# Chunk attention and a multiplicative FFN on one core: 512-column products for part of the first four pairs, and a new hand-written order of loads and steps

## The chip, the cores and the metric

The kernel runs on one core of a Trainium2 chip. The metric is the device time in microseconds of one execution; three executions of the kernel before gave 242.46, 243.07 and 241.17 us, with a median of 242.46 us. A profiled execution is a separate one; all times inside the kernel come from it.

## What is computed

For 8 batches, 8 heads and 576 rows of 64 elements, attention runs inside chunks of 64 rows; the heads are put side by side to rows of 512; then comes a feed-forward part with four weights. Cut to what matters:

```
scores = q_c @ k_c.T / sqrt(64)          # per chunk of 64 rows
attn   = exp(scores) / sum(exp(scores))
x      = (attn @ v_c) as [4608, 512]
a, b   = x @ w1, x @ w2                  # each [4608, 1024]
out    = ((a * b) @ w3) @ w_out          # [4608, 512]
```

The inputs are float32, the products run in bfloat16, and the result is float32. The kernel multiplies w3 by w_out once (w3o), and uses that product for all rows.

## The kernel before, in words

The 4608 rows are 18 **pairs** of 256 rows (p = 0 to 17); two pairs make a **couple** (g = p // 2) of 512 rows. The work is a list of named steps, the string `ORDER`: each step is a letter with its numbers, and a loop at the end of `first_path` calls one small function for each. Every instruction is kept in that order on its engine, so `ORDER` fixes, engine by engine, what stands behind what; semaphores between the engines do the rest. Matrix products are all recorded at L97 and loads at L100, in helpers.

The steps of a pair p, in the order in which the data flow:

- `q`, `k`, `v`: loads from HBM with a cast to bfloat16, issued from POOL's queue (pair 0's q and k come by `R` over the SP and ACT queues as float32 and are cast by ACT in `K`). A pair's q or k is 256 KB in bfloat16, a v too. `i0` to `i3` load quarters of w1 and w2, 256 KB each, `h0`, `h1` halves of w3, `o` all of w_out. POOL's queue holds a limited number of loads: a later one is issued when an earlier one has landed.
- `T p.0`, `T p.1` (L207, DVE): block transposes of q and k.
- `G g.0`, `G g.1` (L199, SP's queue, from pair 6 on): eight transfers inside the chip that spread a couple's transposed q and k over the partitions, so that scores take fewer matmuls.
- `S` (PE): scores, 64 small matmuls, 32 from pair 6 on. `E` (ACT, L240): the exponential. `P` (PE): attention times v, with the row sums as one more column. `N` (DVE, L269 and L272): reciprocal and multiplication, two halves. `X` (DVE, L305 or L313): transposes of the result.
- `H g.0`, `H g.1` (L199, SP's queue, couples 3 to 8): eight transfers that bring a couple's transposed x into place; `A` and `B` of that couple read it.
- `A p.j` and `B p.j` (PE): x @ w1 and x @ w2. From pair 4 on one step makes 128 of the 1024 columns (f = j) for both pairs of the couple: 4 matmuls of 512 columns, written under the couple's even pair. For pairs 0 to 3 one step makes 256 columns (f = 2j and 2j+1) for one pair: 8 matmuls of 256 columns. `C` (ACT, L370) copies the first product out of PSUM, `M` (DVE, L387) multiplies it by the second.
- `O` (PE): 16 matmuls with w3o for a pair's output (24 smaller ones for the last). `Y` (ACT, L417) copies it out, `Q` (SP's queue) stores it.

`V` (DVE), `W` (PE) and `Z` (ACT) make w3o. `D` (PE) are matmuls on zeros whose result nobody reads: nine of 512 columns at the start, then twice six. PSUM is four tiles of two banks for all of it, so a step that opens a tile waits for the reader of an older one. SP's queue, too, issues a transfer only when the eighth before it has landed.

The order of the kernel before around what changes, engine by engine:

```
PE:   D(9) S0.0 S0.1 P0.0 P0.1 D(6) S1 D(6) A0.0 P1 B0.0 A0.1 B0.1 A0.2 A1.0 B0.2 A1.1 B1.0 B1.1
      A0.3 S2 B0.3 P2 A1.2 A1.3 B1.2 B1.3 A2.0 B2.0 S3 A2.1 ...
      B4.7 P8 S9 O4 P9 O5 A6.0 ... B6.4 A6.5 S10 B6.5 A6.6 P10 S11 B6.6 A6.7 P11 B6.7 A8.0 ... B8.7 A10.0
DVE:  T0.0.0 T0.1.0 T0.0.1 T0.1.1 T1.0 N0.0 T1.1 N0.1 X0.0 X0.1 N1.0 X1.0 N1.1 M0.0 X1.1 M0.1 M0.2 T2.0 T2.1
      M1.0 M1.1 M0.3 N2.0 N2.1 X2.0 X2.1 T3.0 T3.1 ...
      M4.3 T10.1 M4.4 X7.1 M4.5 M4.6 M4.7 T11.0 N8.0 N8.1 T11.1 T12.0 X8.0 N9.0 ...
POOL: v0 q1 k1 i0 v1 i1 i2 q2 k2 i3 v2 q3 k3 q4 v3 k4 h0 o h1 q5 k5 v4 q6 k6 q7 k7 q8 v5 k8 q9 k9 q10 v6 v7
      k10 v8 q11 v9 k11 q12 k12 ...
SP:   G3 Q0 Q1 G4 Q2 Q3 H3 G5 H4 G6 Q4 H5 Q5 G7 H6 G8 ...
```

Of the kernel before, what the change touches and what calls it, by code (L numbers as in the profile page):

```python
# [7 lines left out]

ORDER = """
R0.0 R1.0 R0.1 R1.1 v0 D0.0.1.9.512 K0.0 K1.0 T0.0.0 K0.1 T0.1.0 K1.1 S0.0 T0.0.1 E0.0 T0.1.1 q1 k1  # L10
S0.1 i0 E0.1 P0.0 P0.1 T1.0 D0.1.0.6.512 v1 N0.0 T1.1 N0.1 X0.0 X0.1 i1 i2 S1 E1 D1.0.0.6.512 A0.0
C0.0 P1 B0.0 q2 N1.0 X1.0 N1.1 A0.1 C0.1 k2 B0.1 M0.0 A0.2 X1.1 A1.0 i3 C0.2 B0.2 M0.1 A1.1 v2 q3
B1.0 B1.1 M0.2 C1.0 C1.1 T2.0 k3 A0.3 C0.3 T2.1 S2 E2 B0.3 M1.0 M1.1 P2 M0.3 N2.0 N2.1 A1.2 C1.2
X2.0 A1.3 X2.1 C1.3 T3.0 B1.2 q4 T3.1 v3 k4 B1.3 A2.0 M1.2 C2.0 B2.0 S3 E3 T4.0 A2.1 M1.3 B2.1 M2.0
P3 A2.2 h0 N3.0 N3.1 B2.2 X3.0 A2.3 C2.1 C2.2 X3.1 o M2.1 C2.3 B2.3 A3.0 C3.0 M2.2 B3.0 V0 h1 A3.1
A3.2 q5 k5 C3.1 M2.3 B3.1 B3.2 v4 V1 C3.2 q6 T4.1 V2 V3 M3.0 W0 S4 k6 q7 M3.1 Z0 M3.2 V4 V5 W1 T5.0
Z1 W2 V6 V7 T5.1 W3 T6.0 E4 k7 q8 v5 Z2 A3.3 k8 q9 k9 Z3 S5 T6.1 T7.0 q10 T7.1 E5 v6 v7 C3.3 P4 B3.3
N4.0 X4.0 M3.3 O0 G3.0 N4.1 k10 Y0 G3.1 T8.0 O1 X4.1 P5 T8.1 Y1 O2 Q0 N5.0 N5.1 X5.0 v8 X5.1 A4.0 S6
E6 T9.0 T9.1 S7 B4.0 T10.0 Y2 q11 O3 C4.0 M4.0 Q1 E7 P6 v9 N6.0 A4.1 N6.1 C4.1 Y3 B4.1 A4.2 X6.0
M4.1 G4.0 A4.3 X6.1 C4.2 P7 N7.0 C4.3 B4.2 G4.1 k11 B4.3 N7.1 X7.0 A4.4 M4.2 B4.4 Q2 M4.3 C4.4 T10.1  # L20
M4.4 A4.5 C4.5 S8 B4.5 A4.6 C4.6 A4.7 E8 B4.6 Q3 C4.7 X7.1 B4.7 M4.5 q12 P8 H3.0 M4.6 S9 H3.1 M4.7
O4 E9 T11.0 Y4 P9 N8.0 O5 k12 N8.1 A6.0 B6.0 Y5 T11.1 G5.0 T12.0 A6.1 X8.0 N9.0 B6.1 C6.0 C6.1 T12.1
A6.2 q13 X8.1 B6.2 N9.1 X9.0 M6.0 k13 C6.2 v10 T13.0 v11 X9.1 M6.1 A6.3 M6.2 q14 G5.1 C6.3 A6.4 q15
B6.3 C6.4 B6.4 A6.5 S10 C6.5 B6.5 T13.1 M6.3 M6.4 A6.6 H4.0 E10 P10 H4.1 M6.5 S11 N10.0 B6.6 k14
N10.1 v12 A6.7 C6.6 E11 G6.0 P11 M6.6 N11.0 B6.7 X10.0 N11.1 A8.0 A8.1 B8.0 G6.1 C6.7 C8.0 B8.1 A8.2
B8.2 C8.1 M6.7 T14.0 q16 A8.3 M8.0 C8.2 M8.1 X10.1 M8.2 X11.0 Q4 q17 T14.1 H5.0 B8.3 C8.3 S12 S13
X11.1 A8.4 E12 C8.4 B8.4 k15 H5.1 M8.3 E13 v13 k16 A8.5 B8.5 P12 M8.4 k17 v14 T15.0 N12.0 N12.1 O6
A8.6 v15 C8.5 C8.6 T15.1 Y6 T16.0 B8.6 A8.7 M8.5 C8.7 P13 Q5 M8.6 B8.7 X12.0 A10.0 C10.0 B10.0 N13.0
N13.1 M8.7 G7.0 A10.1 T16.1 C10.1 A10.2 X12.1 X13.0 M10.0 C10.2 G7.1 B10.1 B10.2 A10.3 B10.3 C10.3
M10.1 T17.0 A10.4 C10.4 M10.2 M10.3 A10.5 T17.1 B10.4 M10.4 X13.1 v16 H6.0 S14 C10.5 S15 G8.0 B10.5  # L30
M10.5 O7 G8.1 E14 E15 P14 A10.6 H6.1 N14.0 C10.6 B10.6 A10.7 N14.1 Q6 Y7 M10.6 P15 N15.0 N15.1 C10.7
X14.0 S16 B10.7 M10.7 O8 E16 Q7 A12.0 B12.0 C12.0 M12.0 Y8 A12.1 C12.1 P16 S17 N16.0 X14.1 B12.1 E17
A12.2 M12.1 B12.2 A12.3 C12.2 A12.4 B12.3 X15.0 B12.4 v17 C12.3 M12.2 A12.5 N16.1 B12.5 M12.3 H7.0
X15.1 A12.6 X16.0 A12.7 C12.4 M12.4 C12.5 M12.5 C12.6 P17 N17.0 Q8 B12.6 B12.7 M12.6 H7.1 A14.0
A14.1 C12.7 B14.0 N17.1 C14.0 M12.7 O9 B14.1 C14.1 Y9 A14.2 X16.1 M14.0 M14.1 C14.2 A14.3 B14.2 Q9
O10 B14.3 X17.0 H8.0 Y10 Q10 A14.4 C14.3 A14.5 X17.1 C14.4 B14.4 M14.2 B14.5 H8.1 M14.3 A14.6 O11
Y11 B14.6 M14.4 O12 C14.5 C14.6 Y12 A14.7 M14.5 A16.0 C14.7 C16.0 Q11 M14.6 B14.7 A16.1 C16.1 A16.2
B16.0 B16.1 M14.7 M16.0 C16.2 M16.1 Q12 A16.3 O13 B16.2 B16.3 A16.4 C16.3 M16.2 Y13 M16.3 C16.4
A16.5 A16.6 B16.4 A16.7 C16.5 B16.5 M16.4 O14 Y14 C16.6 B16.6 C16.7 M16.5 B16.7 M16.6 Q13 M16.7 O15
Y15 O16 Q14 Q15 Y16 Q16 O17  # L40
"""


# [5 lines left out]
def first_path(  # L49
# [46 lines left out]
    def mm(*a, **kw):
        return inorder(nc.tensor.matmul(*a, **kw))  # L97
# [276 lines left out]
    def do_M(p, j):  # L374
        g = p // 2
        if g not in ab_t:
            ab_t[g] = msb.tile([P, FO, GT], bf, tag="ab", bufs=3, name="ab")
# [9 lines left out]
        inorder(nc.vector.tensor_mul(o, view(a_t.pop((p, j))[:]), view(ps_t.pop((p, j))[:, 1, :])))  # L387
# [201 lines left out]
```

## Time and profile before

| | before |
|---|---|
| time of the profiled execution | 241.66 us |
| its span, first to last instruction | 240.1 us |
| median of three other executions | 242.46 us |
| PE busy | 230.6 us (96%) |
| DVE busy | 152.3 us (63%) |
| ACT busy | 84.7 us (35%) |
| loads by POOL's queue (software) | 18.88 MB, 84.8% of 16 DMA engines' span |
| mean granted PE clock | 0.985 |

In the profile, PE's busy time counts overlapping matmuls and modelled ends, so a busy PE can still be a waiting one: what a step costs is read from the distance between the starts of steps. "qkm<-qkT" are the transfers `G`, "xt<-xm" the transfers `H`, "w<-in_moe_w_dram" the loads of w1, w2 and w3. PEld is PE's weight load. A chain of waits follows the last instruction back to what released it.

### The profile page before, as it was taken

How to read it: one execution, taken by the hardware profiler on the slowest of the kernel's cores; microseconds unless marked ns; L12 is line 12 of the kernel's file. 1: busy time of each engine (PE TensorE's matmuls, PEld its weight loads, DVE VectorE, ACT ScalarE, POOL GpSimd, SP SyncE). 2: the span in 40 equal slices, each digit the busy share in tenths (PEclk: the TensorE clock that was granted, in tenths of full speed). 3: DMA queues.
4: the chain of work that ended last, by engine and by line, in shares of the span. 5: the costliest groups of instructions: out<-in, count | busy, mean ns of one | idle time of the engine just before them, and what ended most of it. 6: DMA issues, size and time to landing. Idle time of an engine off the chain costs nothing.

```text
span 240.1 us, 6225 instructions
## 1 busy us (share of the span) xinstructions
PE 230.6 (96%) x2621; PEld 120.2 (50%) x2621; DVE 152.3 (63%) x237; ACT 84.7 (35%) x119; POOL 83.4 (35%) x112
## 2 busy tenths in 40 slices
PE   5699999999999999999999999999999999999994
PEld 1367788744645444444544444454444444444442
DVE  2766799959979596998599798474773222223200
ACT  4322334214412544333526143355332213521322
POOL 7846865647852424775543520000000000000000
PEclk9679999999999999999999999999999999999999
DMA  6999999999999999999999999860410442202224
GB/s 177 179 185 188 178 175 199 202 188 174 174 220 242 236 224 253 201 204 196 212 222 222 214 252 152 190 210 3 131 48 3 131 131 87 90 0 89 85 90 175
DMA packets 94397, 39.21 MB, mean 163 GB/s; under 512 B 75296, under 2 KB 86816, under 8 KB 94368
## 3 DMA queue, kind: packets, MB, share of 16 engines
q0 software_dynamic: 82592, 18.88, 84.8%
q1 hardware_dynamic: 10720, 19.41, 27.6%
q10 hardware_dynamic: 1056, 0.52, 0.8%
q8 instruction: 20, 0.33, 0.5%
q14 instruction: 9, 0.07, 0.1%
HBM read 38.80 MB, written 9.44 MB: 201 GB/s over the span
## 4 chain that ended last, share of the span: by engine, by line
PE 55%; DMA 31%; POOL 5%; DVE 3%; issue 2%; SPq 2%; ACT 1%; DVEq 0%; POOLq 0%
PE ab_ps L97 34%; PE o_ps L97 17%; DMA qk<-in_k_dram 17%; DMA w<-in_moe_w_dram 7%; DMA qk<-in_q_dram 4%; DMA qkm<-qkT 3%; POOL vbuf L100 2%; SPq L199 2%; PE s_ps L97 2%; POOL qk L100 2%; PE pv L97 2%; DVE ab L387 1%; POOL w L100 1%; DVE xn L272 1%; DVE qkT L207 1%
## 5 line engine op out<-in xcount | busy, mean ns | idle before, releaser
L97 PE MATMUL ab_ps<-xt,w 128*128 128x512 bf16 (+1 forms) x688 | 128.7, 342 | 0.5 <-DMA w<-in_moe_w_dram 0.5
L97 PEld LDWEIGHTS <-w 128*128 128x128 bf16 x704 | 67.0, 98 | 54.9 <-DMA w<-in_moe_w_dram 1.3
L387 DVE TENSOR_TENSOR ab<-a_sb,ab_ps 128x512 bf16<-128x512 f32 x71 | 47.0, 673 | 53.8 <-PE ab_ps L97 30.2
L370 ACT COPY a_sb<-ab_ps 128x512 f32<-128x512 f32 x71 | 41.4, 587 | 73.8 <-PE ab_ps L97 73.0
L97 PE MATMUL o_ps<-w3o,ab 128*128 128x512 bf16 (+2 forms) x296 | 64.8, 373 | 0.5 <-issue 0.3
L207 DVE STREAM_TRANSPOSE qkT<-qk 128x1024 bf16<-128x1024 bf16 (+1 forms) x38 | 45.8, 1232 | 5.5 <-ACT qk L150 3.7
L97 PEld LDWEIGHTS <-ab 128*128 128x128 bf16 x296 | 28.4, 98 | 33.6 <-issue 1.0
L100 POOL DMA_DIRECT2D vbuf<-in_v_dram x40 | 33.8, 847 | 23.2 <-DMA qk<-in_k_dram 5.9
L417 ACT COPY o_sb<-o_ps 128x1024 f32<-128x1024 f32 x17 | 17.2, 1014 | 43.8 <-PE o_ps L97 43.4
L272 DVE TENSOR_TENSOR xn<-pv,rcs 128x512 bf16<-128x512 f32 x36 | 24.9, 691 | 1.2
L100 POOL DMA_DIRECT2D qk<-in_q_dram x23 | 18.0, 783 | 15.8 <-DVE ab L387 4.8
L100 POOL DMA_DIRECT2D qk<-in_k_dram x23 | 17.9, 781 | 11.1 <-DMA qk<-in_k_dram 4.1
L240 ACT ACTIVATE e<-s_ps 128x1024 bf16<-128x1024 f32 (+1 forms) x17 | 16.9, 1000 | 11.4 <-PE s_ps L97 11.2
L313 DVE STREAM_TRANSPOSE xm<-xn 128x512 bf16<-128x512 bf16 x24 | 16.3, 689 | 0.1
L97 PE MATMUL w_ps<-wo,w3T 128*128 128x512 bf16 x64 | 14.1, 379 | 0.1
L269 DVE RECIPROCAL rcs<-pv 128x8 f32<-128x8 f32 x36 | 6.9, 192 | 11.4 <-PE pv L97 11.4
L291 POOL CROSS_LANE_REDUCE all_good<-good 128x1 f32<-128x1 f32 x1 | 0.4, 354 | 39.6 <-DVE both L289 39.6
L100 POOL DMA_DIRECT2D w<-in_moe_w_dram x16 | 11.1, 696 | 5.7 <-DMA w<-in_moe_w_dram 3.9
L97 PEld LDWEIGHTS <-e 64*32 64x32 bf16 (+1 forms) x768 | 7.8, 101 | 6.9 <-issue 4.4
L428 DVE STREAM_TRANSPOSE w3T<-w 128x1024 bf16<-128x1024 bf16 x8 | 9.5, 1210 | 2.4 <-DMA w<-in_moe_w_dram 2.4
L97 PE MATMUL pv<-vbuf,e 64*32 64x65 bf16 (+1 forms) x768 | 10.1, 198 | 0.3 <-ACT e L240 0.2
L97 PEld LDWEIGHTS <-w3T 128*128 128x128 bf16 x64 | 6.1, 98 | 7.5 <-issue 0.4
(28 smaller groups left out, 56.3 us busy)
## 6 DMA issues: line engine op xcount, KB each, us to landing
out_dram<-o_sb SPq DMA_DIRECT2D x17, 512.0 KB, 3.0
qkm<-qkT SPq DMA_DIRECT2D x48, 128.0 KB, 7.0
vbuf<-in_v_dram POOLq DMA_DIRECT2D x32, 128.0 KB, 11.1
w<-in_moe_w_dram POOLq DMA_DIRECT2D x16, 256.0 KB, 9.1
xt<-xm SPq DMA_DIRECT2D x48, 64.0 KB, 5.8
qk<-in_q_dram POOLq DMA_DIRECT2D x11, 256.0 KB, 9.0
qk<-in_k_dram POOLq DMA_DIRECT2D x11, 256.0 KB, 12.1
wo<-in_moe_w_out_dram POOLq DMA_DIRECT2D x4, 256.0 KB, 9.4
```

The source lines that it names most:

```text
L97: return inorder(nc.tensor.matmul(*a, **kw))
L100: return inorder(nc.gpsimd.dma_start(dst, src))
L199: inorder(nc.sync.dma_start(dst, src))
L207: inorder(nc.vector.transpose(qkT_t[g][:, :, p % 2, s, heads(h)].rearrange("p e h (y t) -> p h t e y", t=2), qk_t[p][:, s, heads(h)].rearr ...
L240: inorder(nc.scalar.activation(e_t[p][:, :, heads(hh)], s_t[p, hh][:].rearrange("p u (h q) -> p u h q", q=CH)[:, :, heads(hh)], Exp, scale ...
L269: inorder(nc.vector.reciprocal(rc, pv[:, :, :, D:W]))
L272: inorder(nc.vector.tensor_mul(xn_t[p][:, u], pv[:, :, :, 0:D], rc.to_broadcast([P, 2, 4, D])))
L313: inorder(nc.vector.transpose(xm_t[g][:, u, :, m].rearrange("p o (c y) -> p c o y", y=BL), xn_t[p][:].rearrange("p u r m d -> p (u r) m d" ...
L370: first[p, j] = inorder(nc.scalar.copy(a_t[p, j][:], ps_t[p, j][:, 0, :]))
L387: inorder(nc.vector.tensor_mul(o, view(a_t.pop((p, j))[:]), view(ps_t.pop((p, j))[:, 1, :])))
L417: inorder(nc.scalar.copy(o_sb[:], ps_t.pop(p)[:]))
L428: inorder(nc.vector.transpose(w3T_t[f][:].rearrange("p k (f y) -> p f k y", y=BL), w3[:, NB * f:NB * (f + 1), :].rearrange("p f (k x) -> p ...
```

## The change

Pairs 0 to 3 make only part of their columns pair by pair now; the rest is made for both pairs of the couple at once. Steps with j of 4 and more are the joint ones, and f = j - 4: in couple 0 the joint steps are j = 10 and 11 (f = 6 and 7, the last quarter), in couple 1 they are j = 8 to 11 (f = 4 to 7, the last half). Twelve `A` and `B` steps of 4 matmuls with 512 columns thus stand in place of twelve with 8 matmuls of 256 columns; `C` and `M` keep their number and size.

```
+    def single(p, j):
+        return p < 4 and j < FO // 2
+
     def do_AB(p, j, f, which):
+        if j >= FO // 2 and p < 4:
+            f = j - FO // 2
...
-            if p < 4:
+            if single(p, j):
                 rhs = rhs[:, :, p % 2 * PT:(p % 2 + 1) * PT]
-        fs = (f,) if p >= 4 else (2 * j, 2 * j + 1)
+        fs = (2 * j, 2 * j + 1) if single(p, j) else (f,)
...
     def do_M(p, j):
...
-        if p < 4:
+        if single(p, j):
             o = ab_t[g][:, 2 * j:2 * j + 2, p % 2 * PT:(p % 2 + 1) * PT]
...
         elif p < MOVED:
-            o = ab_t[g][:, j]
+            o = ab_t[g][:, j - FO // 2 if p < 4 else j]
```

`do_D` is written differently and does the same for the numbers used. `ORDER` is new from end to end. Engine by engine, at the places above and where else the steps are followed:

```
PE:   D(9) S0.0 P0.0 S0.1 P0.1 D(6) D(6) S1 P1 A0.0 B0.0 A0.1 B0.1 A0.2 B0.2 A1.0 B1.0 A1.1 A1.2 B1.1 B1.2
      S2 S3 P2 A0.10 A0.11 B0.10 B0.11 A2.0 P3 B2.0 A2.1 B2.1 A3.0 B3.0 A3.1 B3.1 A2.8 A2.9 B2.8 B2.9
      W0 W1 A2.10 W2 W3 S4 S5 B2.10 A2.11 B2.11 O0 P4 O1 P5 O2 S6 O3 A4.0 ...
      B4.7 P8 S9 O4 O5 P9 A6.0 ... A6.6 B6.6 S10 S11 A6.7 P10 B6.7 A8.0 B8.0 A8.1 A8.2 B8.1 O6 B8.2 A8.3
      P11 S12 ... B8.7 O7 A10.0 ... A16.7 B16.7 O12 O13 O14 O15 O16 O17
DVE:  T0.0.0 T0.1.0 T0.0.1 T0.1.1 T1.0 T1.1 N0.0 X0.0 N0.1 X0.1 N1.0 X1.0 M0.0 N1.1 M0.1 X1.1 M0.2 T2.0 M1.0
      T2.1 T3.0 T3.1 M1.1 M1.2 N2.0 N2.1 X2.0 X2.1 M0.10 M0.11 N3.0 N3.1 X3.0 X3.1 M2.0 ...
      M4.5 M4.6 M4.7 N8.0 T10.1 N8.1 X8.0 T11.0 T11.1 T12.0 N9.0 N9.1 X8.1 X9.0 X9.1 T12.1 T13.0 M6.0 ...
      M8.2 N11.0 N11.1 X11.0 M8.3 X11.1 ...
POOL: v0 q1 k1 v1 i0 i1 i2 q2 k2 q3 k3 v2 i3 v3 h0 q4 o h1 q5 k4 k5 q6 q7 k6 q8 k7 k8 v4 q9 v5 k9 q10 v6 v7
      v8 v9 k10 q11 q12 k11 q13 k12 ...
SP:   G3 Q0 Q1 G4 Q2 Q3 H3 G5 H4 Q4 G6 G7.0 H5 Q5 G7.1 Q6 Q7 H6 G8 ...
```

More of the change, by code (lines that the diff above doesn't have):

```diff
@@ L9 @@
 ORDER = """
[L10 to L40, printed above, removed]
+R1.0 R0.0 v0 R0.1 R1.1 q1 k1 v1 i0 i1 D0.0.1.9.512 i2 q2 k2 q3 K0.0 K1.0 K0.1 K1.1 T0.0.0 T0.1.0
@@ new lines @@
+T0.0.1 T0.1.1 T1.0 T1.1 k3 v2 S0.0 E0.0 P0.0 S0.1 E0.1 P0.1 i3 v3 h0 q4 o D0.1.0.6.512 h1 N0.0
+D1.0.0.6.512 q5 X0.0 N0.1 S1 E1 P1 X0.1 A0.0 N1.0 X1.0 B0.0 A0.1 k4 C0.0 B0.1 M0.0 A0.2 N1.1 B0.2
+C0.1 M0.1 C0.2 X1.1 A1.0 B1.0 C1.0 A1.1 M0.2 T2.0 M1.0 T2.1 k5 T3.0 q6 A1.2 T3.1 C1.1 C1.2 B1.1 B1.2
+M1.1 M1.2 S2 E2 S3 P2 N2.0 N2.1 A0.10 C0.10 E3 X2.0 A0.11 B0.10 B0.11 X2.1 A2.0 M0.10 P3 q7 C0.11
+C2.0 M0.11 B2.0 N3.0 N3.1 k6 X3.0 A2.1 X3.1 B2.1 A3.0 B3.0 M2.0 C2.1 M2.1 T4.0 A3.1 C3.0 M3.0 B3.1
+C3.1 M3.1 V0 q8 V1 A2.8 A2.9 B2.8 C2.8 k7 C2.9 V2 V3 B2.9 W0 Z0 W1 k8 M2.8 A2.10 M2.9 V4 v4 V5 W2 V6
@@ new lines @@
+V7 W3 Z1 Z2 Z3 T4.1 T5.0 T5.1 S4 S5 T6.0 T6.1 T7.0 C2.10 T7.1 G3.0 E4 B2.10 M2.10 A2.11 T8.0 T8.1
+G3.1 B2.11 q9 E5 v5 O0 C2.11 P4 M2.11 O1 k9 Y0 Q0 q10 N4.0 T9.0 N4.1 P5 v6 O2 N5.0 Y1 Q1 Y2 v7 v8 S6
+X4.0 X4.1 X5.0 O3 v9 T9.1 G4.0 N5.1 G4.1 E6 X5.1 A4.0 B4.0 C4.0 A4.1 Q2 M4.0 Y3 P6 S7 N6.0 B4.1 C4.1
+M4.1 E7 N6.1 k10 T10.0 q11 q12 Q3 k11 A4.2 A4.3 C4.2 B4.2 C4.3 M4.2 B4.3 M4.3 A4.4 X6.0 P7 S8 N7.0
+X6.1 C4.4 E8 B4.4 A4.5 M4.4 N7.1 C4.5 A4.6 C4.6 B4.5 q13 X7.0 A4.7 k12 X7.1 B4.6 M4.5 M4.6 B4.7 C4.7
@@ new lines @@
+M4.7 H3.0 P8 S9 N8.0 E9 H3.1 T10.1 N8.1 O4 Y4 X8.0 O5 P9 q14 A6.0 T11.0 T11.1 T12.0 N9.0 C6.0 N9.1
+X8.1 X9.0 X9.1 T12.1 Y5 B6.0 G5.0 G5.1 k13 T13.0 k14 H4.0 H4.1 Q4 A6.1 A6.2 C6.1 M6.0 v10 B6.1 M6.1
+C6.2 B6.2 T13.1 M6.2 q15 A6.3 B6.3 C6.3 M6.3 A6.4 B6.4 A6.5 B6.5 C6.4 G6.0 C6.5 M6.4 A6.6 B6.6 C6.6
+M6.5 T14.0 S10 S11 M6.6 E10 A6.7 E11 P10 T14.1 v11 k15 C6.7 B6.7 A8.0 G6.1 N10.0 M6.7 B8.0 A8.1
+T15.0 N10.1 X10.0 X10.1 C8.0 M8.0 A8.2 T15.1 B8.1 q16 O6 C8.1 B8.2 M8.1 C8.2 A8.3 M8.2 Y6 P11 S12
+N11.0 v12 N11.1 G7.0 B8.3 C8.3 v13 X11.0 M8.3 A8.4 A8.5 B8.4 C8.4 A8.6 B8.5 C8.5 X11.1 C8.6 M8.4
@@ new lines @@
+B8.6 M8.5 E12 A8.7 C8.7 M8.6 P12 S13 H5.0 B8.7 E13 N12.0 O7 M8.7 N12.1 H5.1 A10.0 B10.0 A10.1 A10.2
+B10.1 C10.0 B10.2 M10.0 Q5 T16.0 G7.1 C10.1 C10.2 M10.1 Q6 M10.2 Y7 A10.3 P13 S14 X12.0 N13.0 q17
+E14 B10.3 N13.1 X12.1 A10.4 B10.4 X13.0 Q7 k16 X13.1 C10.3 k17 M10.3 C10.4 A10.5 A10.6 C10.5 C10.6
+H6.0 B10.5 v14 v15 v16 v17 H6.1 M10.4 T16.1 T17.0 A10.7 C10.7 T17.1 B10.6 O8 B10.7 M10.5 M10.6 M10.7
+A12.0 Y8 P14 S15 C12.0 N14.0 G8.0 E15 N14.1 B12.0 A12.1 B12.1 M12.0 G8.1 C12.1 M12.1 X14.0 A12.2 P15
@@ new lines @@
+S16 C12.2 N15.0 E16 N15.1 B12.2 X14.1 X15.0 X15.1 A12.3 B12.3 C12.3 M12.2 M12.3 A12.4 B12.4 C12.4
+M12.4 A12.5 B12.5 C12.5 A12.6 B12.6 M12.5 C12.6 M12.6 A12.7 S17 P16 E17 C12.7 H7.0 B12.7 O9 N16.0
+N16.1 X16.0 M12.7 P17 N17.0 N17.1 Q8 Y9 H7.1 A14.0 B14.0 C14.0 M14.0 A14.1 B14.1 C14.1 M14.1 A14.2
+A14.3 B14.2 X16.1 X17.0 X17.1 H8.0 H8.1 B14.3 C14.2 A14.4 M14.2 A14.5 B14.4 B14.5 C14.3 M14.3 A14.6
+C14.4 C14.5 M14.4 M14.5 B14.6 C14.6 M14.6 A14.7 B14.7 C14.7 M14.7 A16.0 A16.1 B16.0 B16.1 Q9 O10 Y10
@@ L41 @@
+C16.0 C16.1 O11 M16.0 A16.2 B16.2 C16.2 M16.1 M16.2 Q10 A16.3 B16.3 C16.3 Y11 M16.3 A16.4 A16.5
+A16.6 B16.4 C16.4 M16.4 B16.5 C16.5 M16.5 B16.6 C16.6 A16.7 B16.7 M16.6 O12 Y12 O13 Q11 Q12 Y13
+C16.7 Q13 O14 Y14 O15 M16.7 Y15 Q14 Q15 O16 Y16 Q16 O17
 """
@@ L326, in do_D @@
     def do_D(which, p, j, n, cols):
-        d, key = ((s_t, (p, (None, 0)[j])), (ps_t, (p, j)), (pv_t, (p, 0)))[which]
+        d, key = ((s_t, (p, 0 if j == 1 else None)), (ps_t, (p, j)), (pv_t, (p, 0)))[which]
         if key not in d:
```

## The prediction

> **What bounds the kernel now.** I read the page first, then the busy times by stage, then the chain of waits, and last the timelines of PE, DVE and SP around the places where the order changes.
>
> ```profile
> PE 230.6 (96%) x2621; PEld 120.2 (50%) x2621; DVE 152.3 (63%) x237; ACT 84.7 (35%) x119; POOL 83.4 (35%) x112
> ```
> ```profile
> 29.50:95.70 66.20, 66.01 (x903) 38.69 (x896) 55.76 (x78) 24.02 (x32) 36.36 (x48) 1.00 1.65 208
> 120.50:236.50 116.00, 115.70 (x901) 53.68 (x900) 57.78 (x95) 40.21 (x59) 10.66 (x14) 1.00 0.62 124
> ```
> ```profile
> 8.35 9.35 DMA w<-in_moe_w_dram
> ...
> 17.98 8.01 DMA w<-in_moe_w_dram
> ...
> 29.57 5.35 PE ab_ps L97 x48
> ...
> 45.25 10.11 DMA qk<-in_k_dram
> ...
> 89.47 10.35 DMA qk<-in_k_dram
> ...
> 117.49 1.83 PE ab_ps L97 x8
> ...
> 204.08 6.91 PE ab_ps L97 x32
> ```
>
> From 29.5 us to the end PE has no hole worth naming (66.01 of 66.20 us, 115.70 of 116.00 us): the end is PE's work plus what PE stood still before 29.5. Before that the chain runs through the weight loads (the last to 26.0 us). One later stretch goes through other hands: a load of k (landed at 99.8), a transpose, and the transfers G of couple 5 (below). That is where I expect the result to be made.
>
> Units from these rows: a matmul of 512 columns takes 6.91/32 = 0.216 us, one of 256 columns 5.35/48 = 0.111, so an A or B step 0.86 and 0.87 to 0.89. From products to attention matmuls and back costs about 0.1 us each way (1.83 for eight matmuls, 1.73 by the unit). The loads i1 second half, i2, q2, k2 and i3 first half, six transfers of 256 KB, landed between 17.70 and 26.00: 1.38 us each.
>
> **The pairing alone.** 96 matmuls of 256 columns become 48 of 512: 48 x (2 x 0.1115 - 0.216) = 0.34 us at most; by the steps in the long PE row 38.22 below (9.03 us to the next start, less W0's wait, for 80 matmuls: 0.1095) it is 0.15. I take 0.15 saved, range 0.1 to 0.35. C and M keep count and size.
>
> **The start.**
>
> ```profile
> 8.95 1.41 PE L97 MATMUL pv<-vbuf,e 64*32 64x65 bf16 x64
> 10.28 2.74 PE L97 MATMUL z_ps<-zero 128*128 128x512 bf16 x6
> ...
> 15.56 1.04 PE L97 MATMUL z_ps<-xt,w 128*128 128x256 bf16 x8
> ...
> 28.87 0.70 PE L97 MATMUL pv<-vbuf,e 64*32 64x65 bf16 x64 [0.16 <-ACT e L240]
> ```
> ```profile
> 14.14 1.02 ACT L240 ACTIVATE e<-z_ps 128x1024 bf16<-128x1024 f32 x1 [4.47 <-PE z_ps L97]
> ```
> ```profile
> 13.68 1.29 DVE L305 STREAM_TRANSPOSE xt<-xn 128x512 bf16<-128x512 bf16 x2
> ...
> 23.93 2.48 DVE L207 STREAM_TRANSPOSE qkT<-qk 128x1024 bf16<-128x1024 bf16 x2
> 26.33 1.24 DVE L387 TENSOR_TENSOR ab<-a_sb,ab_ps 128x512 bf16<-128x512 f32 x2
> ```
> ```profile
> 4.29:7.70 3.41, 1.09 (x35) 0.43 (x33) 2.19 (x4) 2.52 (x5) 3.41 (x6) 1.00 1.82 229
> 7.70:11.12 3.42, 2.59 (x99) 1.72 (x100) 2.09 (x4) 0.94 (x2) 2.88 (x4) 0.50 1.76 184
> 11.12:14.53 3.41, 3.41 (x71) 1.61 (x70) 3.38 (x6) 0.39 (x1) 1.34 (x2) 0.50 1.82 180
> ...
> 17.95:21.36 3.41, 3.11 (x28) 2.31 (x26) 3.29 (x7) 0.58 (x1) 2.20 (x3) 1.00 1.56 191
> ```
>
> P0.0 now stands between S0.0 and S0.1, so S0.1 and with it E0.1 and P0.1 come later: P0.1 ends at about 11.0, not 10.28. All twelve zero matmuls follow it, ahead of S1. At the half clock of 7.70 to 14.53 one takes 0.43 (2.74 for six): eight until 14.5, four more at 0.216, end 15.35. S1 (0.65), then E1 (1.02 and 0.1 on each side) with nothing on PE between, then P1 (0.65), and A0.0 begins at about 18.05; before it began at 15.56, ahead of P1. X0.1 ended at 14.97 and slips by under 0.5, so it is covered; v1, now ahead of i0, costs i0 two half loads, 1.4 us, covered as well.
>
> Most of that delay comes back: before, PE waited for i1, i2 and i3 up to 26.0; now i0 to i2 are in when it wants them. Twelve steps of 0.875 end at 28.55, S2 at 29.2. DVE then sets the pace: after M0.2 (about 24.0) it has T2.0, M1.0, T2.1, T3.0, T3.1, M1.1, M1.2: 4 x 1.24 + 3 x 0.62 = 6.8, end 30.8, and P2 needs the PSUM tile that M1.2 reads. P2 ends at 31.25 against 29.50, with S3 done already. i3 is put behind q3, k3 and v2: 26.0 + 3 x 1.38 = 30.15 and its second half 31.5, hidden behind P2 and A0.10. The stage's sum: 1.75 later, 0.65 of it work done ahead.
>
> **To P8.**
>
> ```profile
> 34.85 0.96 PE L97 MATMUL s_ps<-qkT 32*64 32x64 bf16 x64
> ...
> 38.22 8.91 PE L97 MATMUL ab_ps<-xt,w 128*128 128x256 bf16 x80
> 47.25 3.61 PE L97 MATMUL w_ps<-wo,w3T 128*128 128x512 bf16 x16
> 50.80 0.71 PE L97 MATMUL s_ps<-qkT 32*64 32x64 bf16 x64
> ```
> ```profile
> 95.72 0.45 PE L97 MATMUL pv<-vbuf,e 64*64 64x65 bf16 x32
> ```
>
> P8 began at 95.72. Now: +1.75, -0.65 (S3), -0.15 (pairing), -0.4 (S and P stand in seven groups, not nine: two times in and out), -0.5 (S3 was 0.25 longer than S4, and W0 waited 0.27 for o; k4 moves behind o and h1, so o lands a load earlier), +0.3 (A3.0 has only B2.0, A2.1, B2.1, 2.6 us, to cover N3 and X3). Sum 96.05. The moved loads v4, v8, v9, k4, k6 to k8 are wanted late enough: v4 is the tightest: k5 landed at 55.4 and has the same loads ahead of it now, v4 stands seven loads behind it, 55.4 + 7 x 1.38 = 65.1, and P4 comes at about 68, behind O0; without that cover each further load costs 1.4.
>
> **P8 to A8.0, where it is lost.**
>
> ```profile
> 90.11 1.30 DVE L207 STREAM_TRANSPOSE qkT<-qk 128x1024 bf16<-128x1024 bf16 x1
> ...
> 96.51 1.32 DVE L207 STREAM_TRANSPOSE qkT<-qk 128x1024 bf16<-128x1024 bf16 x1
> 97.72 0.17 DVE L269 RECIPROCAL rcs<-pv 128x8 f32<-128x8 f32 x1
> 97.93 0.69 DVE L272 TENSOR_TENSOR xn<-pv,rcs 128x512 bf16<-128x512 f32 x1
> ...
> 99.92 2.49 DVE L207 STREAM_TRANSPOSE qkT<-qk 128x1024 bf16<-128x1024 bf16 x2 [0.46 <-DMA qk<-in_k_dram]
> ```
> ```profile
> 101.31 5.66 SPq L199 DMA_DIRECT2D qkm<-qkT  x8
> 107.97 6.76 SPq L199 DMA_DIRECT2D xt<-xm  x8
> ```
> ```profile
> xt<-xm SPq DMA_DIRECT2D x8, 64.0 KB, 6.1
> ```
> ```profile
> PEld L97 <- DMA xt<-xm: 0.4, 1, 0.4
> ```
> ```profile
> 119.63 2.12 PE L97 MATMUL ab_ps<-xt,w 128*128 128x512 bf16 x9
> ```
>
> Before, T10.1 (90.11) and T11.0 (96.51) were done when P8's N8.0 began (97.72), and T11.1 (99.92 to 101.2) waited 0.46 for k11. G5 left at 101.31, the moment T11.1 ended; H4, limited to eight transfers in flight, took until 114.7 to issue and landed some 6 us behind its last start, at 120.2; A8.0 started at 120.5 (four matmuls into the last row) and had waited 0.4 for H4. So T11.1, G5, H4, A8.0 is a chain without slack already, and PE's row hides it.
>
> The new order puts T10.1, N8.1, X8.0, T11.0 and T11.1 behind N8.0 on DVE, and N8.0 behind P8. From 96.05: N8.0 starts at 96.4; N 0.85, T 1.23, N 0.92, X 0.62, T 1.23: T11.1 starts at 101.3 and ends at 102.6, 1.4 later than before. k11, one load further back (99.8 + 1.38 = 101.2), is just in. G5 and H4 move by the same 1.4, since loads fill the DMA engines as before: A8.0 at 121.9. PE is ready for it at 119.3 (26 steps and groups from P8 in the units above), so it stands still for 2.6 us. The price is bounded below by what H4 allowed before (A8.0 at 120.5, 0) and above by a k11 that is a further load late (2.8). P11 moves from ahead of A8.0 to behind it (0.4), and three changes fewer between products and attention pay for it: what follows A8.0 is the same work within 0.1 us.
>
> **After A8.0.**
>
> ```profile
> 128.38 0.66 DVE L313 STREAM_TRANSPOSE xm<-xn 128x512 bf16<-128x512 bf16 x1
> ```
> ```profile
> 139.07 2.12 PE L97 MATMUL ab_ps<-xt,w 128*128 128x512 bf16 x9
> ```
>
> H5 lies alike: X11.1 ended at 129.0 and A10.0 began at 139.9, 10.9 later. P11 now stands behind A8.0, six more products and O6 (9.6 us), so it comes at 131.5, and N11, X11.0, M8.3, X11.1 end at 135.6; H5 landed 8.8 after X11.1 before, so 144.4 now, and PE wants A10.0 at 144.1: with the 0.3 from landing to start, 0.6 lost (0 to 1.5). H6 to H8 have two us and more of room. The six outputs in a row at the end need 3.45 us of PE each, and a store is done sooner; the last output ends as before: 0.
>
> **Sum.** 1.4 + 0.1 + 0.6 = 2.1 us later. The profiled execution took 241.66 us, which gives 243.8; the median of the runs is 0.8 above that execution, so I predict 244.6.
>
> **Rivals.** *The transfers are not the bound.* H4 may land by 119.3. For it: 64 KB took a median of 2.0 us once the loads were over.
>
> ```profile
> xt<-xm SPq DMA_DIRECT2D x8, 64.0 KB, 2.0
> ```
>
> Against it: 6.1 us at H4 with loads running, and they still run then. It decides if G5 and H4 together get 2.6 us faster; A8.0 then comes 1.2 earlier than before and H5 is in time: 242.46 - 1.2 + 0.1 = 241.4, not slower. The Trainium skill, "DMA: Bandwidth & Descriptors", section "Anatomy of one DMA", fits 2.0 us plus the bytes over 436 GB/s for a gpsimd transfer, by estimate 2.15 us for 64 KB; by that rule this rival would hold. The row without loads agrees with the page, the row at H4 does not, so the rule gets no more than 0.15.
>
> *The clock drops again.* The window 4.29 to 7.70 had PE busy for 32% and the clock was 0.50 behind it; 91% (17.95 to 21.36) kept it at 1.00. The new window 14.53 to 17.95 has about 2.3 of 3.42 us, 67%, because PE waits for E1 with an empty queue. If that is too little, 3.4 us run at half speed, 1.7 lost, of which DVE's pace before P2 hides 0.8: 244.6 + 0.9 = 245.5. The Trainium skill, "TensorE: Matmul & The Clock Gate", section "What's actually happening", lowers the clock after an idle window of about 3.4 us; 67% is not idle, and by that rule 244.6 stays. The trace is harsher than the rule, since 32% was enough to drop it.
>
> *k11 is late.* v8 and v9 now go ahead of k10, q11 and k11. If the loads between 76 and 101 us, which shared the engines with G, H and stores, run one load behind my count, T11.1 starts 1.4 later, and A8.0 with it: 246.0.
>
> *The order does nothing and only the pairing counts*: 242.46 - 0.15 = 242.3. It speaks for this that PE is full in both; it needs T11.1 to end by 101.2 although P8 is later.
>
> **Numbers.** Chain through H4: 0.50, its own range 243.3 to 245.9 (H4 1.4 with half a load either way, H5 0 to 1.2). In time: 0.15 (241.4). Clock: 0.15 (245.5). k11: 0.12 (246.0). Pairing only: 0.08 (242.3). The range 241.2 to 247.0 reaches to both outer cases with the runs' own spread. What a measurement of this kernel tells from no change is about 1%, 2.4 us: under 240.0 needs the first rival and a better start too, 0.08; over 244.9 takes a good third of the forecast's own chance and most of clock and k11, 0.42; within, 0.50.
>
> **What will show it.** A0.0 near 18.0 instead of 15.6 and A0.10 near 31.2; P8 near 96; T11.1 ending near 102.6; PE's weight load waiting some 2.5 us for xt<-xm once, A8.0 near 121.9; a shorter such wait near 144. The forecast is wrong if A8.0 begins before 120.5, if the clock is under 1.00 after 17.9 us, or if PE waits over 1 us anywhere between 32 and 95.

## The result, and the profile after

| | before | after |
|---|---|---|
| median of 17 runs each | 242.39 us | 244.23 us |
| lowest and highest | 241.17 to 243.30 | 243.12 to 245.52 |
| profiled execution, its span | 241.66, 240.1 | 244.76, 243.2 |
| ratio after / before | | 1.0076, 95% interval 1.0057 to 1.0095 |

The changed kernel is 1.84 us slower by the medians; 244.6 was predicted. The two profiled executions lie 3.1 us apart, because that of before is 0.7 below its median and that of after 0.5 above. Where steps are compared below, that is a comparison of these two executions; prices of a whole edit go by the ratios.

The page of the changed kernel, busy times by engine and the transfers of instructions:

```profile
PE 229.2 (94%) x2555; PEld 115.6 (48%) x2573; DVE 153.1 (63%) x237; ACT 84.8 (35%) x119; POOL 83.4 (34%) x112
...
q8 instruction: 20, 0.33, 0.5%
```

PE is 1.4 us less busy in a span 3.1 longer: 4.5 us of standing still were added. Where, says the timeline of PE (start, length, what, idle time before it and its releaser):

```profile
15.73 0.77 PE L97 MATMUL z_ps<-qkT 32*64 32x64 bf16 x64
17.64 0.70 PE L97 MATMUL pv<-vbuf,e 64*32 64x65 bf16 x64 [1.15 <-ACT e L240]
18.27 1.92 PE L97 MATMUL z_ps<-xt,w 128*128 128x256 bf16 x16
...
31.34 1.04 PE L97 MATMUL ab_ps<-xt,w 128*128 128x512 bf16 x3
```
```profile
35.77 0.25 PE L97 MATMUL pv<-vbuf,e 64*32 64x65 bf16 x15
36.66 0.57 PE L97 MATMUL pv<-vbuf,e 64*32 64x65 bf16 x49 [0.64 <-issue]
```
```profile
97.47 0.45 PE L97 MATMUL pv<-vbuf,e 64*64 64x65 bf16 x32
```
```profile
120.11 1.04 PE L97 MATMUL ab_ps<-xt,w 128*128 128x512 bf16 x4
122.31 1.89 PE L97 MATMUL ab_ps<-xt,w 128*128 128x512 bf16 x8 [1.17 <-DMA xt<-xm]
```
```profile
141.53 3.62 PE L97 MATMUL o_ps<-w3o,ab 128*128 128x512 bf16 x15
145.89 2.32 PE L97 MATMUL ab_ps<-xt,w 128*128 128x512 bf16 x10 [0.74 <-DMA qkm<-qkT]
```

Five places: P1 waits for E1 (1.15), P3 stops in its middle for nothing that the profile shows ("issue", 0.64), P8 begins at 97.47 instead of 95.72, A8.0 waits for a transfer of H4 (1.17), A10.0 for H5 (0.74; the row names qkm, which A10.0 does not read; H5's last transfer landed at 145.44). The chain of waits of the changed kernel (start, length, what):

```profile
116.67 5.51 DMA xt<-xm
...
122.31 4.48 PE ab_ps L97 x20
...
135.37 6.53 DMA xt<-xm
141.91 3.93 DMA qkm<-qkT
145.89 6.20 PE ab_ps L97 x28
```

Both handovers, H4 and H5, are on it, where the chain of before had neither. The timelines of DVE and of SP's queue show how the first one came to be late:

```profile
98.25 0.20 DVE L269 RECIPROCAL rcs<-pv 128x8 f32<-128x8 f32 x1
98.48 0.69 DVE L272 TENSOR_TENSOR xn<-pv,rcs 128x512 bf16<-128x512 f32 x1
99.09 1.30 DVE L207 STREAM_TRANSPOSE qkT<-qk 128x1024 bf16<-128x1024 bf16 x1
...
101.86 3.63 DVE L207 STREAM_TRANSPOSE qkT<-qk 128x1024 bf16<-128x1024 bf16 x3
```
```profile
104.38 4.98 SPq L199 DMA_DIRECT2D qkm<-qkT  x8
110.67 6.58 SPq L199 DMA_DIRECT2D xt<-xm  x8
...
134.82 5.71 SPq L199 DMA_DIRECT2D xt<-xm  x8
```

T10.1 (99.09) and the three transposes from 101.86 (T11.0, T11.1, T12.0) stand behind N8.0 now. T11.1 ended at 104.32 (101.25 before) and G5 left at 104.38 (101.31 before).

The granted clock changes at 9.08 and 15.91 us in this execution, not at 7.71 and 14.53 as before. The windows around S1 and P1, cut there (window and length, busy time of PE, PEld, DVE, ACT and POOL, granted clock, DMA share, GB/s):

```profile
12.49:15.91 3.42, 3.42 (x20) 1.09 (x22) 2.91 (x6) 0.00 (x0) 1.71 (x3) 0.50 1.45 198
15.91:19.32 3.41, 2.27 (x138) 1.99 (x133) 1.11 (x3) 1.02 (x1) 1.87 (x3) 1.00 1.45 195
19.32:22.73 3.41, 3.41 (x34) 3.06 (x32) 2.68 (x6) 1.17 (x2) 2.31 (x4) 1.00 1.70 185
```

PE was busy for 67% of the window with the hole ahead of P1, and the clock behind it is 1.00.

### The profile page after: what moved, and what is told of

Read it like the earlier page. It is cut to its first block, busy times and chain, and to the rows that moved or that the text cites. A ratio compares the mean times of both kernels' runs of the same rounds, so it can differ in the third digit from the quotient of the medians.

```text
span 243.2 us, 6107 instructions
## 1 busy us (share of the span) xinstructions
PE 229.2 (94%) x2555; PEld 115.6 (48%) x2573; DVE 153.1 (63%) x237; ACT 84.8 (35%) x119; POOL 83.4 (34%) x112
## 4 chain that ended last, share of the span: by engine, by line
PE 81%; DMA 9%; DVE 4%; issue 2%; ACT 1%; SPq 1%; POOL 0%; DVEq 0%; POOLq 0%
PE ab_ps L97 43%; PE o_ps L97 24%; PE w_ps L97 6%; DMA xt<-xm 5%; PE z_ps L97 3%; PE pv L97 3%; DMA vbuf<-in_v_dram 2%; PE s_ps L97 2%; DMA qkm<-qkT 2%; DVE ab L393 1%; DVE xn L272 1%; ACT e L240 1%; SPq L199 1%; POOL vbuf L100 0%; DVE xt L305 0%
## 5 line engine op out<-in xcount | busy, mean ns | idle before, releaser
L97 PE MATMUL ab_ps<-xt,w 128*128 128x512 bf16 (+1 forms) x634 | 125.8, 355 | 2.8 <-DMA xt<-xm 1.2
L97 PEld LDWEIGHTS <-w 128*128 128x128 bf16 x656 | 62.5, 98 | 60.9 <-DMA out_dram<-o_sb 1.6
L97 PE MATMUL o_ps<-w3o,ab 128*128 128x512 bf16 (+2 forms) x285 | 63.4, 373 | 0.8 <-DVE ab L393 0.2
L207 DVE STREAM_TRANSPOSE qkT<-qk 128x1024 bf16<-128x1024 bf16 (+1 forms) x38 | 45.1, 1228 | 5.3 <-ACT qk L150 3.8
L313 DVE STREAM_TRANSPOSE xm<-xn 128x512 bf16<-128x512 bf16 x24 | 15.8, 691 | 0.2
L97 PE MATMUL z_ps<-zero 128*128 128x512 bf16 x20 | 9.1, 631 | 1.6 <-DVE zero L116 1.4
```

Source lines behind the costliest of these rows:

```text
L207: inorder(nc.vector.transpose(qkT_t[g][:, :, p % 2, s, heads(h)].rearrange("p e h (y t) -> p h t e y", t=2), qk_t[p][:, s, heads(h)].rearr ...
L313: inorder(nc.vector.transpose(xm_t[g][:, u, :, m].rearrange("p o (c y) -> p c o y", y=BL), xn_t[p][:].rearrange("p u r m d -> p (u r) m d" ...
```

## The experiments

Theory 1 is the prediction's: the time is lost at the handovers through H4 and H5. The rivals changed as results came in. Each ratio is to the kernel before on the same chip; the changed kernel's own is 1.0076.

**1. The first handover undone.** DVE, in the changed kernel:

```
-M4.5 M4.6 M4.7 N8.0 T10.1 N8.1 X8.0 T11.0 T11.1 T12.0
+M4.5 T10.1 M4.6 M4.7 T11.0 N8.0 N8.1 T11.1 X8.0 T12.0
```

> The changed kernel, with T10.1 and T11.0 back ahead of N8.0 and T11.1 ahead of X8.0 on DVE, as before; nothing else. Theory 1 (the chain T11.1, G5, H4, A8.0 carries the loss): T11.1 ends near 102.8 instead of 104.3 us, H4 lands 1.0 to 1.5 earlier, PE's wait at A8.0 (1.3 us in the changed kernel's trace) shrinks to 0.3 or less, and the time is 0.8 to 1.3 us below the changed kernel's, that is 0.5 to 1.0 us above the kernel before. Rival (H4 is paced by the loads that share the engines, not by its start): H4 lands where it did, and the time stays within 0.3 us of the changed kernel's, 1.8 us above before.

Measured: 243.49 us (7 runs), ratio 1.0067 (1.0042 to 1.0091). By the ratio that is no difference from the changed kernel that the runs can tell. SP's queue and PE in its trace:

```profile
102.53 4.98 SPq L199 DMA_DIRECT2D qkm<-qkT  x8
108.83 6.96 SPq L199 DMA_DIRECT2D xt<-xm  x8
```
```profile
145.45 1.89 PE L97 MATMUL ab_ps<-xt,w 128*128 128x512 bf16 x8 [1.68 <-DMA qkm<-qkT]
```

G5 and H4 leave 1.85 earlier, and A8.0 begins at 121.04 with no wait, 1.27 earlier. But A10.0 begins only 0.44 earlier, and waits for H5 for 1.68 instead of 0.74. The gain was taken by the next handover.

**2. The start eased.** The second six zero matmuls behind E1, so that S1 comes 2.2 us earlier and the zeros fill the hole ahead of P1:

```
-P0.1 D(6) D(6) S1 P1 A0.0
+P0.1 D(6) S1 D(6) P1 A0.0
```

> The changed kernel, with the second six zero matmuls behind S1, as before, instead of ahead of it. A0.0 starts near 16.2 us instead of 18.3 in both theories. Theory 1: the head start survives in part: DVE's four transposes of pairs 2 and 3 and k3's landing (27.4) allow P2 only 0.5 to 0.9 us earlier, P8 follows, A8.0 follows P8, and the time falls by 0.5 to 0.9 us against the changed kernel. Rival (the stage up to 30 us is paced by loads and DVE alone): A0.10 stays at 31.3 and the time does not move by more than 0.3 us.

Measured: 244.16 us (6 runs), ratio 1.0081 (1.0053 to 1.0109): nothing. A0.0 came at 16.75 and A0.10 0.68 earlier, but P8 at 97.54. The head start ends at S6, in the timeline of PE:

```profile
77.00 0.21 PE L97 MATMUL s_ps<-qkm 64*64 64x64 bf16 x1
77.67 0.76 PE L97 MATMUL s_ps<-qkm 64*64 64x64 bf16 x31 [0.46 <-DMA qkm<-qkT]
```

S6 waits for G3. My statement that P8 follows A0.10 was wrong.

**3. The pairing undone.** The changed order, with the joint steps made as single ones (0.10 and 0.11 as 0.3 and 1.3; 2.8 to 2.11 as 2.2, 3.2, 2.3, 3.3):

```
-A0.10 C0.10 E3 X2.0 A0.11 B0.10 B0.11 ... A2.8 A2.9 B2.8
+A0.3 C0.3 E3 X2.0 A1.3 B0.3 B1.3 ... A2.2 A3.2 B2.2
```

> The changed kernel's order with its twelve joint steps of four 512-column matmuls made again as steps of eight 256-column matmuls, at the same places. Theory 1 (the order carries the loss, the pairing is worth 0.15 us): 0.1 to 0.35 us slower than the changed kernel. Rival (the pairing itself costs, since a joint step needs both pairs' x and gives its columns in one piece): faster than the changed kernel by 0.5 us or more.

Measured: 246.65 us (6 runs), ratio 1.0178 (1.0148 to 1.0207). Undoing the pairing costs 2.4 us against the changed kernel, not 0.15. PE does not lose it in longer matmuls but standing still. Its timeline:

```profile
36.94 0.28 PE L97 MATMUL ab_ps<-xt,w 128*128 128x256 bf16 x1 [1.19 <-issue]
...
69.07 2.75 PE L97 MATMUL o_ps<-w3o,ab 128*128 128x512 bf16 x12 [1.75 <-issue]
...
77.01 0.30 PE L97 MATMUL pv<-vbuf,e 64*32 64x65 bf16 x28 [0.62 <-issue]
```

These stalls have no releaser: PE stops in the middle of a group, and the profile shows nothing that it waits for. Counting PE's instructions in program order (matmuls, weight loads and the few others) gives each stall a number, good to about two:

| kernel | step, how late | number | remainder by 256 |
|---|---|---|---|
| before | S3 0.24, O6 0.46 | 1218, 3778 | 194, 194 |
| after | P3 0.81, S6 0.36 | 1219, 2244 | 195, 196 |
| unpaired | S3 0.42, A2.0 1.36, O0 1.91 | 962, 1219, 1986 | 194, 195, 194 |
| unpaired | P5 0.79, S8 0.30 | 2243, 2755 | 195, 195 |

Always the same place in a block of 256, and the profile's queue "instruction" moves 20 blocks of 16 KB (0.33 MB); the page counts it on the same 16 DMA engines as the loads. That gave theory F: PE gets its instructions 256 at a time, and where it runs through a block faster than the next one arrives, it stops. In the changed kernel the block that ends in P3 holds 5.6 us of work; its successor's 16 KB moved from 34.10 to 35.22 and PE went on at 36.66. An attention group of 64 matmuls spends 128 instructions in 0.65 us, a step of four products with 512 columns only 8 in 0.86. Experiment 8 tests it.

**4. The late loads left out.**

```
     def load_qk(p, which, h=None):
+        if p >= 13:
+            qk_t[p] = qk_t[p - 5]
+            return
...
         vb_t[p] = vb_free.pop(0)
+        if p >= 10:
+            return
```

> The changed kernel without the loads of q and k of pairs 13 to 17 and of v of pairs 10 to 17: these pairs use older data, so the output is not the reference's. Loads end near 104 us instead of 150. Theory 1: the transfers G5 and H4 then land in 2 to 3 us instead of 6, PE's waits at A8.0 (1.3) and A10.0 (0.9) go, and the time falls by 1.8 to 2.5 us, to about the kernel before or just under. Rival (PE's waits there come from the order of the steps, whatever the transfers take): the waits stay over 0.5 us each and the time falls by less than 1 us.

Measured: 242.02 us (10 runs), ratio 1.0000 (0.9979 to 1.0021). The transfers H in its page (median from issue to landing in the last column), and PE at A10.0:

```profile
xt<-xm SPq DMA_DIRECT2D x48, 64.0 KB, 2.0
```
```profile
143.69 1.67 PE L97 MATMUL ab_ps<-xt,w 128*128 128x512 bf16 x7
```

T11.1 ended as late as in the changed kernel (104.50), but H4's last transfer, issued at 115.06 and at 2.0 us, landed near 117.1 (122.18 in the changed kernel, 116.67 + 5.51 in its chain), and neither A8.0 (121.14) nor A10.0 waits. With the loads out of the way, the late transposes cost nothing: they are a loss because the transfers behind them share the DMA engines with the loads.

**5. The late transposes alone, in the kernel before.**

```
 DVE, kernel before
-M4.3 T10.1 M4.4 X7.1 M4.5 M4.6 M4.7 T11.0 N8.0 N8.1 T11.1 T12.0 X8.0
+M4.3 M4.4 X7.1 M4.5 M4.6 M4.7 N8.0 T10.1 N8.1 X8.0 T11.0 T11.1 T12.0
```

> The kernel before, with one thing of the new order: on DVE the steps around P8 stand as in the changed kernel (N8.0, T10.1, N8.1, X8.0, T11.0, T11.1) instead of T10.1 and T11.0 ahead of N8.0. Nothing else differs from the kernel before. Theory 1 (the prediction's chain T11.1, G5, H4, A8.0 sets the time there): T11.1 ends about 1.2 later, at 102.4 instead of 101.25; H4 lands and A8.0 begins 1.0 to 1.2 later, at 121.6 instead of 120.5, and as PE is full from there to the end, the last output and the time are 1.0 to 1.2 later, ratio 1.004 to 1.005. Rival (the head start of PE, lost before P8, is what counts, and H4 has hidden slack): A8.0 stays within 0.3 of 120.5 and the time within 0.3 of the kernel before.

Measured: 242.62 us (12 runs), ratio 1.0024 (1.0009 to 1.0039): 0.6 us, between the two theories. In the trace T11.1 ends 1.67 later (102.92), and A8.0 begins 0.93 later. P8 itself came 0.35 later. A part of the delay is made up on the way through the transfers. (The profiled execution took 244.28, well above its median, and what it lost later is not used here.)

**6. Both handovers early.** Experiment 1, and P11 and H5 brought forward:

```
 PE
-B8.1 O6 B8.2 A8.3 P11 S12 B8.3
+B8.1 P11 B8.2 O6 A8.3 S12 B8.3
 DVE
-T15.0 N10.1 X10.0 X10.1 M8.0 T15.1 M8.1 M8.2 N11.0 N11.1 X11.0 M8.3 X11.1
+N10.1 X10.0 X10.1 M8.0 M8.1 N11.0 N11.1 M8.2 X11.0 X11.1 T15.0 T15.1 M8.3
 SP
-G7.0 H5.0 H5.1 Q5
+H5.0 H5.1 G7.0 Q5
```

> The changed kernel with T10.1 and T11.0 ahead of N8.0 again (as in the first experiment, which ended at 243.49 against 244.23 with A10.0 still 1.84 late for H5), and in addition with P11 taken from behind O6 to behind B8.1, T15.0 and T15.1 moved behind it on DVE, and X11.0, X11.1 and H5 following at once. Theory 1 (the two handovers through H4 and H5 hold all of the change's loss that lies behind P8): X11.1 ends near 131 instead of 134.7, H5 lands near 140.5, A10.0 begins at about 143.5 without a wait, and the last output starts 1.8 to 1.9 earlier than in the first experiment, near 234.0: 241.6 on the runs, the kernel before's time within 0.4. Rival (PE loses elsewhere what it does not wait for H5, because DVE is crowded or outputs wait for PSUM tiles): A10.0 at 144.5 or later and 242.6 or more.

Measured: 242.57 us (12 runs), ratio 1.0011 (0.9988 to 1.0035). H5 and A10.0 in its trace:

```profile
129.39 4.95 SPq L199 DMA_DIRECT2D xt<-xm  x8
```
```profile
140.19 3.62 PE L97 MATMUL o_ps<-w3o,ab 128*128 128x512 bf16 x15
143.65 1.67 PE L97 MATMUL ab_ps<-xt,w 128*128 128x512 bf16 x7
```

A10.0 follows O7 directly, 2.24 earlier than in the changed kernel, as theory 1 said (143.5); the median is 1.0 above its figure. The two edits together take the ratio from 1.0076 to 1.0011, though the first alone was worth nothing that could be measured. The second alone was not run. P8 stays as late in this kernel and in experiment 4 (97.65) as in the changed one.

**7. And the start eased as well** (experiments 6 and 2 together).

> As the run before it, and the second group of six zero matmuls behind E1 as well, which on its own gave A0.10 0.68 earlier and nothing behind P8. If the handover G3, S6 swallows that head start again, this run equals the one before it within 0.2. If some of it survives, it is up to 0.7 earlier (241.0).

Measured: 242.43 us (12 runs), ratio 1.0020 (1.0003 to 1.0037), the same as experiment 6. P2 came at 30.05 instead of 30.43, P8 at 97.70 instead of 97.65: G3 and S6 swallow the head start again.

**8. Block boundaries moved.** 64 small matmuls more at the start, nothing else:

```
+        rows = 32 if cols < 512 else P
...
-            mm(d[key][:, 0, 0:cols], lhsT=zero[:, 0:P], rhs=zero[:, 0:cols], start=True, stop=True)
+            mm(d[key][0:2 * rows if rows < P else P, 0, 0:cols], lhsT=zero[0:rows, 0:min(2 * rows, P)],
+               rhs=zero[0:rows, 0:cols], start=True, stop=True)
...
-D0.0.1.9.512
+D0.0.1.9.512 D0.0.1.64.64
```

> The changed kernel with 64 more small matmuls on zeros (32x64, nobody reads them) right behind the first nine, where PE stands idle until 6.6 us. No step is added, left out or moved behind them; only every later instruction of PE has a number higher by 128, so that each boundary of 256 instructions falls 128 instructions earlier in the work. Theory F (the stalls without a releaser come from refilling PE's instructions in blocks of 256, and a refill takes 4 to 6.5 us while loads run): the block that now ends in P2 holds only 1.9 us of work and the one that ends in S5 only 1.4 us, so PE stands still there for some 2.1 to 4.5 us and for 2.6 to 5 us, the stalls of 0.6 in P3 and of 0.36 in S6 go away, and the time is 3.5 to 8 us longer: 248 to 252. Rival (the stalls belong to the steps P3 and S6, to their operands or PSUM banks): they stay where they are and the time stays at 244.2 within 0.5.

Measured: 250.31 us (4 runs), ratio 1.0329 (1.0293 to 1.0366). PE's timeline, with windows as above:

```profile
32.73 0.53 PE L97 MATMUL pv<-vbuf,e 64*32 64x65 bf16 x39
37.21 0.40 PE L97 MATMUL pv<-vbuf,e 64*32 64x65 bf16 x25 [3.94 <-issue]
...
38.36 5.47 PE L97 MATMUL ab_ps<-xt,w 128*128 128x512 bf16 x22 [0.22 <-issue]
43.77 0.70 PE L97 MATMUL pv<-vbuf,e 64*32 64x65 bf16 x64
```
```profile
30.98:34.39 3.41, 1.85 (x167) 1.41 (x167) 2.91 (x5) 1.02 (x1) 1.94 (x3) 1.00 1.83 180
34.39:37.81 3.42, 0.60 (x26) 0.36 (x27) 0.13 (x1) 0.00 (x0) 1.47 (x3) 0.50 1.48 195
37.81:41.22 3.41, 3.19 (x8) 1.21 (x8) 1.98 (x4) 1.56 (x3) 2.00 (x4) 0.50 1.48 200
```
```profile
69.03 1.27 PE L97 MATMUL s_ps<-qkT 32*64 32x64 bf16 x128
```

PE stops for 3.94 us in the middle of P2, again at instruction 1219, which now stands there; P3 and S6 run through. The stalls go with the number and not with the step: theory F holds, the rival falls. Up to P8, 6.87 later: 2.0 at the start, for the small matmuls lasted until 8.66 and not 6.6 as I had meant; 4.2 in P2; 1.8 in the products after it, seven of which start 0.43 apart instead of 0.22, for behind the stop the granted clock was 0.50 (34.39 to 41.22); less 1.2 for P3 and S6. So the 1.8 is a second price of the same stop, one that theory F had not counted. Theory F's second stall, in S5, did not come: S4 and S5 run through in 1.27. The 16 KB for the block behind moved at 65.12, while PE still worked at W2 and W3, 3.9 us ahead of S4. So the request is not made when PE's arithmetic crosses a boundary but ahead of it, and by how much is open.

**9. O3 ahead of S6,** in the kernel of experiment 7.

```
-O2 S6 O3 A4.0
+O2 O3 S6 A4.0
```

> The run with both handovers early and the second zero matmuls behind E1 (242.43 on the runs), with one more step moved: O3 stands ahead of S6 on PE, so that S6 no longer waits for G3. If S6's wait for G3 is what swallowed the head start of 0.6, then A4.0 begins 0.8 earlier (81.2 instead of 81.98), P8 begins near 96.9 instead of 97.7, and A8.0 and the end follow by what H4 lets through, 0.3 to 0.7: 241.7 to 242.1. Rival (the next handover holds: k11 lands at 100.3 and H4 at 120, whatever PE gained): P8 earlier, but A8.0 within 0.2 of 121.2 and the time at 242.4 within 0.2.

Measured: 242.68 us (12 runs), ratio 1.0023 (1.0000 to 1.0046), no faster. In its trace S6 no longer waits:

```profile
75.72 4.26 PE L97 MATMUL o_ps<-w3o,ab 128*128 128x512 bf16 x19
79.91 0.45 PE L97 MATMUL s_ps<-qkm 64*64 64x64 bf16 x32
80.29 2.76 PE L97 MATMUL ab_ps<-xt,w 128*128 128x512 bf16 x11
```

P8 came at 96.06 instead of 97.70, and A8.0 began at 120.61 instead of 121.18. Of 1.64 us, 0.57 reached A8.0 in that execution, and nothing shows in the median of the runs. Half of the lead was gone at A6.0 (105.32 instead of 106.11), ahead of H4. DVE's and PE's timelines around P8:

```profile
95.27 1.32 DVE L207 STREAM_TRANSPOSE qkT<-qk 128x1024 bf16<-128x1024 bf16 x1 [0.77 <-DMA qk<-in_k_dram]
```
```profile
97.19 0.45 PE L97 MATMUL s_ps<-qkm 64*64 64x64 bf16 x32 [0.69 <-DVE ab L393]
```

T10.1, which stands ahead of M4.6 since experiment 1's edit, waits for k10 (landed at 95.25), M4.6 and M4.7 come behind it, and S9 waits for DVE. What was left met H4, which landed at 120.48; k11 landed at 100.81, and T11.1 ended at 102.15 instead of 102.65. Neither forecast holds as written: the theory's time was missed, and the rival had A8.0 within 0.2 of 121.2. What is left of the rival is that later handovers took the gain, first a load of k and then H4. No version beat the kernel before.

## Why the prediction was right, and where not

**The forecast case is what happened.** T11.1, G5, H4 and A8.0 became a chain that PE waits for, then X11.1, H5 and A10.0; experiments 4 and 6 take the handovers' waits away, one by the loads and one by the order, and both end at the time of before within their intervals (1.0000 and 1.0011, each give or take some 0.5 us). To that precision the 1.84 us lie there.

**The start: right.** A0.0 at 18.27 (18.05 predicted, where the terms named add up to 17.87), A0.10 at 31.34 (31.25), PE idle while it waits for E1. P2 was said to wait for M1.2 on DVE, and its second half did: M1.2 ended at 30.98 (30.8 predicted). Its first half waited for E2 on ACT, which the prediction had not named:

```profile
28.93 0.68 PE s_ps L97 x64
29.63 1.03 ACT e L240
30.66 0.04 issue
30.71 0.32 PE pv L97 x32
31.04 0.37 PE pv L97 x32
```

The two waits ended 0.3 us apart, so it made no difference to the number.

**To P8: 1.4 us too early.** Predicted 96.05, measured 97.47. The sum prices every group and product at the units of its rows, and that step failed: 1.17 of the 1.42 are the stalls in P3 and S6, which the new order brought by setting S2, S3, P2 and P3 within one block and a part of 256 instructions. Nothing in the prediction allowed for stalls without a releaser, although S3's 0.25 extra stood in it as an oddity of S3; by its number (1218) it was the same stall.

**The pairing: right sign, wrong size and reason.** 0.15 us was its worth by matmul times. In the new order it is 2.4 us, since undoing it puts 96 more instructions into the stretch before P6: the stalls in the unpaired kernel sum to 4.48 up to P5, against 1.17 in the changed one, and P8 comes 3.24 later. The 2.4 us belong to this order: the 96 instructions also move the boundaries, and experiment 8 shows that this alone can cost near 5 us (6.87 at P8, less the 2.0 at the start). How much is the number of instructions and how much the place of the boundaries was not separated, and what the pairing would be worth in the old order was not tried.

**H4: right mechanism, size 1.3 too large.** PE's wait at A8.0 was forecast as 2.6 and is 1.33 by the starts of steps. PE came later than thought (P8), and T11.1 too (104.32 for 102.6), yet A8.0 began at 122.31, only 0.4 behind the forecast. The term that was mis-sized is "G5 and H4 move by the same 1.4": from T11.1's end to A8.0 it took 19.26 us before, 18.52 in experiment 5, 17.99 after. A later start was partly made up, as experiment 5 shows too, with 0.6 us for 1.2 expected. That error and the one at P8 partly cancel: A8.0 was to come 1.4 later than before, and came 1.8 later.

**H5: right.** 0.6 predicted, 0.9 measured by the starts (144.98 wanted, 145.89 begun). But the prediction put H4's loss and H5's side by side and added them. Experiment 1 shows that they are one behind the other: taking away the first leaves nearly the whole sum, because PE then waits longer at the second.

**The nearness of the number is partly luck.** For the profiled execution the prediction gave 243.8, and it took 244.76, 3.1 more than before instead of 2.1. The 0.8 added for the runs made up for it: the median of the changed kernel lies 0.5 below its profiled execution, not above.

**The rivals.** The transfers were the bound (A8.0 waited 1.17). The clock did not drop a second time at 67% busy, though the window lay elsewhere than predicted. What the half clock at the start costs, the runs do not show; the mean granted clock of an execution does not tell, for that of experiment 4 is 1.00, and its zero matmuls too start 0.43 apart up to 13.8 us. k11 landed at 100.55, and DVE came to T11.1 at 103.05. "Only the pairing counts" fell with the result.

## What to carry to other kernels

A gain ahead of a handover that is bound elsewhere is kept only until that handover: to price an edit, list the next two or three places where PE meets a transfer and ask at each what remains, and do not add up waits that lie behind one another. Where transfers between two engines share DMA with a stream of loads, put whatever starts them ahead of work that is not urgent. Where an engine stops without a releaser, number its instructions before looking for a cause in the step.
